# Subtracting, exponentiating and summing the first ten units of an attention on ScalarE, one activation per head

## The chip, the cores and the metric

The kernel runs on one core of a Trainium2 chip. Its engines are TensorE (PE; PEld is its weight load), VectorE (DVE), ScalarE (ACT), GpSimd (POOL) and SyncE (SP), which issues every DMA here. Each engine takes its instructions in the order of its own queue; semaphores hold an instruction until what it needs is there. The metric is the device time of one execution in microseconds (us), the median of three runs.

## The reference

An attention over pooled keys and values feeds two feed-forward layers (q and k come with a spread of 0.8, v of 0.1):

```python
# q, k, v: (8, 8, 576, 64) = batch, heads, tokens, head_dim
k_p = k.reshape(B, H, 72, 8, D).mean(axis=3)
v_p = v.reshape(B, H, 72, 8, D).mean(axis=3)
scores = np.matmul(q, k_p.transpose(0, 1, 3, 2)) / np.sqrt(D)
scores = scores - np.max(scores, axis=-1, keepdims=True)
attn = np.exp(scores)
attn = attn / (np.sum(attn, axis=-1, keepdims=True) + 1e-09)
x = np.matmul(attn, v_p)              # -> (4608, 512) tokens x model
h = x @ w_in;  x = (h * np.cos(h)) @ w_out        # d_ff = 2048
h = x @ w2_in; out = (h * np.clip(h + 3, 0, 6) / 6) @ w2_out
```

## The kernel before

All work is in fp32. Each large matmul is made of three products of parts: a tensor is split in a rounded high part (`xh`, `wh`, `gh`, `pth`) and a low part (`xl`, `wl`, `gl`, `ptl`), so that four matmuls of 128x512 times three products make one step of a layer's half. The weights come as 64-bit words and are turned into fp32 by DVE with four instructions per half (`convert_weights`, L116 to L128), rounded on ACT (L133) and split on POOL (L134).

The attention goes through *units*: 8 batches of 576 tokens, each cut into four units of 128 tokens and one of 64, 40 in all, each with 8 heads of 72 keys. For a unit:

- `unit_q` (L389) turns the queries: four PE transposes and a copy on ACT into `qT` (L395).
- `unit_s` (L401), once for each half of four heads: two score matmuls (L407) into a PSUM bank (`ap_ps`), DVE takes each head's maximum into `mx` (L416) and subtracts it into `e` in SBUF (L418). `mx` and the bank have two buffers each.
- `unit_exp` (L420): one exponent on ACT over all 576 columns of `e` (L423), with the scores' factor 1/(sqrt(64) x 8) as its scale.
- `unit_norm` (L425): DVE sums each head into `sm` (L429), adds 1e-9 (L430) and takes the reciprocal (L431); POOL multiplies (L433) and copies the last columns (L435).
- `unit_pt` (L443) turns `e` on PE (L459), copies the high part on ACT (`pth`, L463) and takes the low part on DVE (`ptl`, L464). `pv` (L485) multiplies with the values (L494) and an ACT copy and a DMA bring the result into `x_d` (L502, L503).

For each batch keys and values are loaded into one buffer (`raw`), summed by eights on DVE or POOL (L334, L338; the values of batch 1 on POOL), and the keys are turned and copied by ACT into `kbd` (`make_kbd`, L345), from which the score matmuls read.

Then come the 144 + 144 *steps* of the feed-forward layers, `gemm1` (L175) into `h`, a chain of ACT and DVE instructions to `g` (in the first layer L185, L195, L196, the sine L199, L209), `gh` (L212), `gl` (L218), and `gemm2` (L237). A step of the first layer begins once the first 512 tokens of `x_d` are there. The attention is a generator in *pieces*; units 0 to 9 or so run before and around the first step, the others between the steps, by a table of goals (`GOFF`). The queues are not in the order of the code: a scheduler sorts the instructions by due times of its own as the program is built, so that a change of one unit moves its neighbours as well.

ACT reads its functions from tables. The sine and the exponent are in different ones, and a load (ACT_TABLE_LOAD) stands ahead of each change; the copies need none.

Of the kernel before, what the change touches and what calls it, by code (L numbers as in the profile page):

```python
# [8 lines left out]
F32 = mybir.dt.float32  # L9
# [3 lines left out]
AF = mybir.ActivationFunctionType  # L13
ALU = mybir.AluOpType
AX = mybir.AxisListType
# [3 lines left out]
POOL = 8  # L19
MAGIC = 12582912.0  # L20
INV_2PI = 1.0 / (2.0 * math.pi)
TWO_PI = 6.283185


def f(ap):
# [4 lines left out]
def tile_kernel(ctx, tc, q, k, v, wi1, wo1, wi2, wo2, ident_d, mask_d, out):  # L30
    nc = tc.nc
    B, H, S, D = q.shape
    NT, DM = out.shape
    P = 128
    N = 512
    SP = S // POOL
# [153 lines left out]
    def chain1(s):  # L190
# [3 lines left out]
        if m == 0:  # L194
# [3 lines left out]
            )  # L198
            nc.scalar.activation(out=g, in_=g, func=AF.Sin, scale=-TWO_PI)  # L199
        else:  # L200
# [65 lines left out]
    ap = actx.enter_context(tc.tile_pool(name="ap", bufs=1))  # L266
# [6 lines left out]
    raw, kp = {}, {}  # L273
    kbd = [ap.tile([P, NP, 2 * SP], F32, name=f"kbd{n}") for n in range(2)]
    NE = 4
    ebuf = [ap.tile([P, H * SP + P], F32, name=f"e{n}") for n in range(NE)]
    raw_t = ap.tile([P, KC, POOL * D], F32, name="raw")
    qm, qT, pts = {}, {}, {}

    def part_of(b, i):  # L280
        return [u1 > i for _, u1 in PARTS[b]].index(True)
# [4 lines left out]
    def piece(kind):  # L286
        turn = turns[kind] = turns.get(kind, -1) + 1
        if started:
            return ps_a.tile([P, N], F32, tag="ap", name="ap_ps", bufs=2)
        tag = SKIND[kind][turn % len(SKIND[kind])]  # L290
        if tag == "ap":
            return ps_a.tile([P, N], F32, tag="ap", name="ap_ps", bufs=2)
        if tag == "h":
            return ps_h.tile([P, N], F32, tag="h", name="h")
        return ps_y.tile([P, N], F32, tag=tag, name=tag)
# [45 lines left out]
    def make_kbd(b, part):  # L341
        kt = kp[b, "k"]
        ps = piece("q")
        kb = kbd[b % 2]
        cp = lambda o, i_: nc.scalar.activation(out=o, in_=i_, func=AF.Copy)  # L345
        if part == 0:
            for c in range(KFULL):
                nc.tensor.transpose(
                    ps[:, c * P : (c + 1) * P], kt[:, c].rearrange("p e d -> p (e d)"), ident
                )  # L350
            full = (KFULL * P) // (2 * SP)
            cp(
                kb[:D, :full, :SP],
                ps[:D, : full * 2 * SP].rearrange("p (j x) -> p j x", x=2 * SP)[:, :, :SP],
            )
            cp(
                kb[D:, :full, SP:],
                ps[D:, : full * 2 * SP].rearrange("p (j x) -> p j x", x=2 * SP)[:, :, SP:],
            )
            o = full * 2 * SP  # L360
            cp(kb[:D, full, :SP], ps[:D, o : o + SP])
            cp(kb[D:, full, SP : KFULL * P - o], ps[D:, o + SP : KFULL * P])
        else:
            nc.tensor.transpose(
                ps[:, :KREM], kt[:KREM, KFULL].rearrange("p e d -> p (e d)"), ident[:KREM, :KREM]
            )
            cp(kb[D:, NP - 1, 2 * SP - KREM :], ps[D:, :KREM])
# [33 lines left out]
    def unit_s(n, half):  # L401
        b, i = divmod(n, NU)
        w = UNITS[i][1]
        ps = piece("s")
        t = qT[n]
        for j in range(2):
            nc.tensor.matmul(  # L407
                ps[:w, j * 2 * SP : (j + 1) * 2 * SP],
                t[:, 2 * half + j, :w],
                kbd[b % 2][:, 2 * half + j, :],  # L410
                start=True,
                stop=True,
            )
        s3 = ps[:w, : 4 * SP].rearrange("p (g s) -> p g s", s=SP)
        mx = ap.tile([P, 4, 8], F32, tag="mx", name="mx", bufs=2)[:, :, 0:1]
        nc.vector.tensor_reduce(out=mx[:w, :, 0], in_=s3, op=ALU.max, axis=AX.X)  # L416
        e = ebuf[n % NE][:w, half * 4 * SP : (half + 1) * 4 * SP].rearrange("p (g s) -> p g s", s=SP)
        nc.vector.tensor_tensor(out=e, in0=s3, in1=mx[:w].to_broadcast([w, 4, SP]), op=ALU.subtract)  # L418

    def unit_exp(n):  # L420
        w = UNITS[n % NU][1]
        e = ebuf[n % NE][:w, : H * SP]
        nc.scalar.activation(out=e, in_=e, func=AF.Exp, scale=1.0 / (math.sqrt(D) * POOL))  # L423

    def unit_norm(n):  # L425
        w = UNITS[n % NU][1]
        e = ebuf[n % NE][:w, : H * SP].rearrange("p (h s) -> p h s", s=SP)
        sm = ap.tile([P, H, 4], F32, tag="sm", name="sm", bufs=2)[:, :, 0:1]
        nc.vector.tensor_reduce(out=sm[:w, :, 0], in_=e, op=ALU.add, axis=AX.X)  # L429
        nc.vector.tensor_scalar(out=sm[:w], in0=sm[:w], scalar1=1e-9, scalar2=None, op0=ALU.add)  # L430
        nc.vector.reciprocal(out=sm[:w], in_=sm[:w])  # L431
        eng = nc.vector if n in ND else nc.gpsimd
        eng.tensor_tensor(out=e, in0=e, in1=sm[:w].to_broadcast([w, H, SP]), op=ALU.mult)  # L433
        e = ebuf[n % NE][:w]
        eng.tensor_copy(  # L435
            out=e[:, H * SP :].rearrange("p (t j x) -> p t j x", t=2, x=VR),
            in_=pairs_of(e)[:, :, P:].unsqueeze(1).to_broadcast([w, 2, NP, VR]),
        )

    def pairs_of(e):  # L440
        return e[:, : H * SP].rearrange("p (j x) -> p j x", x=2 * SP)

    def unit_pt(n):  # L443
# [11 lines left out]
        ps = piece("p")  # L455
        e = ebuf[n % NE][:w]
        kc = NP if w == P else KC
# [49 lines left out]
    def attention():  # L507
        units = B * NU
        normed = finished = 0
        for n in range(units + 3):  # L510
            b, i = divmod(n, NU)
            if n < units:
                unit_s(n, 0)
                yield
                unit_s(n, 1)
                unit_exp(n)
                yield
                if n + 3 < units:
                    load_q(n + 3)
                if n + 1 < units:  # L520
                    unit_q(n + 1)
                    yield
            if n < units and b + 1 < B:
                if i == 2:
                    pool_kv(b + 1, "k", nc.vector if KD[b + 1] else nc.gpsimd)
                    load_kv(b + 1, "v")
                if i == 4:
                    make_kbd(b + 1, 0)
                    yield
                    make_kbd(b + 1, 1)  # L530
                    yield
            while normed < units and n - normed >= NL[normed // NU]:
                unit_norm(normed)
                normed += 1
# [25 lines left out]
    for bl in range(NB):  # L560
        n = NAL[bl]
        steps += [(0, (0, bl), bl, fc, fc == 0, fc == n - 1) for fc in range(n)]
    SA = len(steps)
    for bl in range(NB):
        n = NAL[bl]
# [15 lines left out]
    pool_kv(0, "k", nc.vector, K0S)  # L581
    load_kv(0, "v")
    make_kbd(0, 0)
    make_kbd(0, 1)
    unit_q(0)
# [75 lines left out]
    for slot in range(2 * (T + LAG) + 4):  # L661
# [3 lines left out]
        if not odd and s < T:  # L665
# [9 lines left out]
            if key[0] == 1 and fc == NF - 5:  # L675
                for c in range(NC):
                    t = ypl.tile([P, N], F32, tag="yv", name="yv", bufs=4)
                    nc.sync.dma_start(
                        out=t, in_=yp_d[c * P : (c + 1) * P, bl * N : (bl + 1) * N]
# [95 lines left out]
```

## Time and profile before

| | before |
|---|---|
| median of three runs (lowest to highest) | 1800.62 us (1800.45 to 1802.0) |
| the profiled execution | 1801.62 us |
| its span, first to last instruction | 1799.8 us |
| PE busy | 1739.2 us, 97% |
| DVE / ACT / POOL busy | 896.4 / 891.6 / 393.8 us |
| mean granted TensorE clock | 0.986 of full speed |

A row of the trace names a line, an engine, an operation, and what is written from what is read; then how many, their busy time, the mean of one in ns, and the idle time of the engine just before them with what ended it. Idle time is put down to whatever came last. Engine times overlap, so a sum of busy times is not a time of the program; what an engine's work is worth is read stage by stage.

### The profile page before, as it was taken

The page shows a single profiled execution, that of the slowest core. Times are in us where ns is not written, and L with a number is a line of the kernel's source. Part 1 is how long each engine was busy: PE and PEld are TensorE (multiplying, and loading weights), DVE is VectorE, ACT ScalarE, POOL GpSimd, SP SyncE. Part 2 cuts the span into 40 slices and gives each one's busy share as a digit, 9 for nine tenths or more (in the row PEclk, how much of TensorE's full clock was granted, in tenths as well). Part 3 has the DMA queues.
Part 4 walks back from the last instruction along what each step waited for, and adds up shares of the span by engine and source line. Part 5 has one row for each costly group of instructions (what it writes and reads, how often), then busy time and mean ns, then how long its engine had stood idle before and what let it go on. Part 6 is the DMA issues. An engine that isn't in the chain of part 4 may idle for free.

```text
span 1799.8 us, 21002 instructions
## 1 busy us (share of the span) xinstructions
PE 1739.2 (97%) x7952; PEld 1429.5 (79%) x7952; DVE 896.4 (50%) x1398; ACT 891.6 (50%) x1508; POOL 393.8 (22%) x320
## 2 busy tenths in 40 slices
PE   5689999999999999999999999999999999999999
PEld 4567777788888888888888788888888888888887
DVE  6998656656777656654446852222222222222222
ACT  3588878787666655555556543232323222232222
POOL 2755444222223222221112421010101000010000
PEclk7799999999999999999999999999999999999999
DMA  7656442323333313222223411010101010100000
GB/s 196 194 172 195 143 136 74 118 83 103 117 105 118 106 59 105 97 85 76 71 70 106 140 59 47 1 47 1 47 1 48 0 47 8 40 18 24 0 24 24
DMA packets 115077, 139.84 MB, mean 78 GB/s; under 512 B 44192, under 2 KB 68896, under 8 KB 114976
## 3 DMA queue, kind: packets, MB, share of 16 engines
q1 hardware_dynamic: 114976, 138.51, 24.8%
q8 instruction: 62, 1.02, 0.2%
q14 instruction: 39, 0.32, 0.1%
HBM read 100.73 MB, written 37.75 MB: 77 GB/s over the span
## 4 chain that ended last, share of the span: by engine, by line
PE 85%; DVE 6%; DMA 3%; POOL 2%; ACT 2%; issue 2%; SPq 0%; DVEq 0%; POOLq 0%; ACTq 0%
PE y L237 40%; PE h L175 40%; PE ap_ps L494 1%; PE ap_ps L407 1%; DVE raw L334 1%; DMA raw<-in_k_dram 1%; DMA raw<-in_v_dram 1%; POOL xl L153 1%; DVE sm L429 1%; DVE g L196 1%; POOL e L433 1%; DVE a L125 1%; PE ap_ps L393 0%; PE ap_ps L459 0%; DVE sm L430 0%
## 5 line engine op out<-in xcount | busy, mean ns | idle before, releaser
L175 PE MATMUL h<-xl,wh 128*128 128x512 f32 x1152 | 451.3, 392 | 4.2 <-POOL xl L153 4.2
L175 PE MATMUL h<-xh,wh 128*128 128x512 f32 x1152 | 453.5, 394 | 0.5 <-DVE g L209 0.5
L175 PE MATMUL h<-xh,wl 128*128 128x512 f32 x1152 | 450.8, 391 | 0.0
L201 DVE SCALAR_TENSOR_TENSOR g<-g,h 128x512 f32<-128x512 f32 x144 | 99.3, 689 | 454.7 <-ACT g L187 454.7
L153 POOL TENSOR_TENSOR xl<-xr,xh 128x512 fp32r<-128x512 f32 x108 | 153.3, 1438 | 779.2 <-ACT xh L152 778.1
L187 ACT ACTIVATE g<-h,bias_c 128x512 f32<-128x512 f32 x144 | 99.0, 687 | 409.7 <-PE h L175 409.3
L218 DVE TENSOR_TENSOR gl<-g,gh 128x512 fp32r<-128x512 f32 x255 | 190.3, 746 | 157.7 <-ACT gh L212 154.4
L212 ACT ACTIVATE gh<-g 128x512 fp32r<-128x512 f32 x288 | 181.6, 630 | 175.2 <-DVE g L201 104.5
L175 PEld LDWEIGHTS h<-xl,wh 128*128 128x128 f32 x1152 | 216.7, 188 | 50.2 <-POOL xl L153 6.5
L175 PEld LDWEIGHTS h<-xh,wh 128*128 128x128 f32 x1152 | 216.9, 188 | 45.5 <-issue 1.2
L175 PEld LDWEIGHTS h<-xh,wl 128*128 128x128 f32 x1152 | 216.9, 188 | 44.3
L237 PE MATMUL y<-gh,wh 128*128 128x512 f32 x576 | 226.7, 394 | 0.0
L237 PE MATMUL y<-gl,wh 128*128 128x512 f32 x576 | 226.6, 393 | 0.0
L237 PE MATMUL y<-gh,wl 128*128 128x512 f32 x576 | 225.6, 392 | 0.0
L237 PE MATMUL y<-wh,gh 128*128 128x512 f32 x576 | 224.3, 389 | 1.1 <-DVE yv L245 1.1
L237 PE MATMUL y<-wh,gl 128*128 128x512 f32 x576 | 224.1, 389 | 0.0
L237 PE MATMUL y<-wl,gh 128*128 128x512 f32 x576 | 224.1, 389 | 0.0
L196 DVE SCALAR_TENSOR_TENSOR g<-g,t 128x512 f32<-128x512 f32 x144 | 112.6, 783 | 149.8 <-ACT g L195 149.5
L134 POOL TENSOR_TENSOR wl<-a,wh 128x512 fp32r<-128x512 f32 x64 | 88.4, 1381 | 269.4 <-ACT wh L133 269.4
L237 PEld LDWEIGHTS y<-wh,gh 128*128 128x128 f32 x576 | 108.2, 188 | 24.4 <-DVE yv L245 1.9
L199 ACT ACTIVATE g<-g 128x512 f32<-128x512 f32 x144 | 91.0, 632 | 72.9 <-DVE g L196 72.5
L237 PEld LDWEIGHTS y<-wh,gl 128*128 128x128 f32 x576 | 108.1, 188 | 22.5
(110 smaller groups left out, 2086.1 us busy)
## 6 DMA issues: line engine op xcount, KB each, us to landing
xr<-x_d SPq DMA_DIRECT2D x72, 256.0 KB, 3.2
st<-in_moe_w_in_dram SPq DMA_DIRECT2D x32, 512.0 KB, 6.6
st<-in_moe_w_out_dram SPq DMA_DIRECT2D x32, 512.0 KB, 4.1
yp_d<-ys SPq DMA_DIRECT2D x36, 256.0 KB, 2.4
yv<-yp_d SPq DMA_DIRECT2D x36, 256.0 KB, 3.4
xr<-y_d SPq DMA_DIRECT2D x36, 256.0 KB, 2.7
out_dram<-ys SPq DMA_DIRECT2D x36, 256.0 KB, 2.0
raw<-in_k_dram SPq DMA_DIRECT2D x8, 1024.0 KB, 5.7
```

The source lines that it names most:

```text
L125: nc.vector.scalar_tensor_tensor(out=a, in0=hi, scalar=0xC0000000, in1=a, op0=ALU.bitwise_and, op1=ALU.bitwise_or)
L134: nc.gpsimd.tensor_tensor(out=wl, in0=w, in1=f(wh), op=ALU.subtract)
L153: nc.gpsimd.tensor_tensor(out=xl, in0=t, in1=f(xh), op=ALU.subtract)
L175: nc.tensor.matmul(h, a[:, cs], z, start=(n == 0), stop=(n == 3 * NC - 1))
L187: nc.scalar.activation(out=g, in_=hs[s], func=AF.Relu, bias=bias_c[:, 2:3], scale=1.0)
L196: mark[s] = nc.vector.scalar_tensor_tensor(out=g, in0=g, scalar=MAGIC, in1=t, op0=ALU.subtract, op1=ALU.subtract)
L199: nc.scalar.activation(out=g, in_=g, func=AF.Sin, scale=-TWO_PI)
L201: mark[s] = nc.vector.scalar_tensor_tensor(out=g, in0=g, scalar=6.0, in1=h, op0=ALU.min, op1=ALU.mult)
L212: nc.scalar.activation(out=gh, in_=g, func=AF.Copy)
L218: eng.tensor_tensor(out=gl, in0=gs[s][0], in1=f(gh), op=ALU.subtract)
L237: nc.tensor.matmul(y[c], a, z, start=(first and n == 0), stop=(last and n == 2))
L334: eng.tensor_tensor(out=t[:, :, :w], in0=t[:, :, :w], in1=t[:, :, w : 2 * w], op=ALU.add)
```

## The change

In units 0 to 9 (`HX`) the subtract, the exponent and the sum become one activation for each head, exp(-score + mx) with `mx` as bias column and the sum written into `sm` by the activation itself. An activation can only add its bias, so the scores must come with the other sign: the copies into `kbd` multiply by `S_SCALE` = -1/64 and DVE takes the minimum instead of the maximum, which is the negative maximum. From unit 10 on the subtract, the exponent over 576 columns and the sum stay as they were, with a scale of -1. `sm` has four buffers instead of two, and lives from the first half of the scores on.

```diff
+S_SCALE = -1.0 / 64.0
...
+    HX = range(10)
...
-        cp = lambda o, i_: nc.scalar.activation(out=o, in_=i_, func=AF.Copy)
+        cp = lambda o, i_: nc.scalar.activation(out=o, in_=i_, func=AF.Copy, scale=S_SCALE)
...
-        nc.vector.tensor_reduce(out=mx[:w, :, 0], in_=s3, op=ALU.max, axis=AX.X)
+        nc.vector.tensor_reduce(out=mx[:w, :, 0], in_=s3, op=ALU.min, axis=AX.X)
         e = ebuf[n % NE][:w, half * 4 * SP : (half + 1) * 4 * SP].rearrange("p (g s) -> p g s", s=SP)
-        nc.vector.tensor_tensor(out=e, in0=s3, in1=mx[:w].to_broadcast([w, 4, SP]), op=ALU.subtract)
+        if n in HX:
+            if half == 0:
+                sums[n] = ap.tile([P, H, 4], F32, tag="sm", name="sm", bufs=4)[:, :, 0:1]
+            for g in range(4):
+                nc.scalar.activation(
+                    out=e[:, g],
+                    in_=s3[:, g],
+                    func=AF.Exp,
+                    bias=mx[:w, g],
+                    scale=-1.0,
+                    accum_out=sums[n][:w, half * 4 + g],
+                )
+        else:
+            nc.vector.tensor_tensor(
+                out=e, in0=s3, in1=mx[:w].to_broadcast([w, 4, SP]), op=ALU.subtract
+            )
 
     def unit_exp(n):
+        if n in HX:
+            return
         w = UNITS[n % NU][1]
         e = ebuf[n % NE][:w, : H * SP]
-        nc.scalar.activation(out=e, in_=e, func=AF.Exp, scale=1.0 / (math.sqrt(D) * POOL))
+        nc.scalar.activation(out=e, in_=e, func=AF.Exp, scale=-1.0)
...
-        sm = ap.tile([P, H, 4], F32, tag="sm", name="sm", bufs=2)[:, :, 0:1]
-        nc.vector.tensor_reduce(out=sm[:w, :, 0], in_=e, op=ALU.add, axis=AX.X)
+        if n in HX:
+            sm = sums.pop(n)
+        else:
+            sm = ap.tile([P, H, 4], F32, tag="sm", name="sm", bufs=4)[:, :, 0:1]
+            nc.vector.tensor_reduce(out=sm[:w, :, 0], in_=e, op=ALU.add, axis=AX.X)
```

The scheduler's order on the engines, with the line numbers of each kernel (those of the changed one are larger by 1 to 22), at two places. A name such as e_96 is one of the four buffers of `e`. DVE before, from the first maximum, units 0 and 1:

```order
L416 TENSOR_REDUCE mx<-ap_ps 128x4 x2
L418 TENSOR_TENSOR e_96<-ap_ps,mx 128x288 x2
L416 TENSOR_REDUCE mx<-ap_ps 128x4
L334 TENSOR_TENSOR raw<-raw 128x5x256
L429 TENSOR_REDUCE sm<-e_96 128x8
L334 TENSOR_TENSOR raw<-raw 128x5x128
L430 TENSOR_SCALAR sm<-sm 128x8
L418 TENSOR_TENSOR e_97<-ap_ps,mx 128x288
L338 TENSOR_TENSOR vt<-raw 128x320
L431 RECIPROCAL sm<-sm 128x8
```

and after, at the same place:

```order
L418 TENSOR_REDUCE mx<-ap_ps 128x4 x2
L336 TENSOR_TENSOR raw<-raw 128x5x256
L452 TENSOR_SCALAR sm<-sm 128x8
L418 TENSOR_REDUCE mx<-ap_ps 128x4
L336 TENSOR_TENSOR raw<-raw 128x5x128
L453 RECIPROCAL sm<-sm 128x8
L340 TENSOR_TENSOR vt<-raw 128x320
L418 TENSOR_REDUCE mx<-ap_ps 128x4
```

The subtracts and the sum are gone, and the reciprocal of unit 0 has come ahead of the last sum of the values. ACT before, around unit 9 (e_97, 64 tokens) and the first steps:

```order
L423 ACTIVATE e_97<-e_97 64x576
L185 ACTIVATE t<-h 128x512
L395 ACTIVATE qT<-ap_ps 128x512
L195 ACTIVATE g<-t 128x512
L345 ACTIVATE kbd_94<-ap_ps 64x3x72 x2
L345 ACTIVATE kbd_94<-ap_ps 64x72
L345 ACTIVATE kbd_94<-ap_ps 64x8
L345 ACTIVATE kbd_94<-ap_ps 64x64
L185 ACTIVATE t<-h 128x512
L199 ACT_TABLE_LOAD
L199 ACTIVATE g<-g 128x512
```

and after:

```order
L424 ACTIVATE e_97,sm<-ap_ps,mx 64x72
L186 ACTIVATE t<-h 128x512
L424 ACTIVATE e_97,sm<-ap_ps,mx 64x72
L196 ACTIVATE g<-t 128x512
L424 ACTIVATE e_97,sm<-ap_ps,mx 64x72 x3
L200 ACT_TABLE_LOAD
L200 ACTIVATE g<-g 128x512
L424 ACT_TABLE_LOAD
L424 ACTIVATE e_97,sm<-ap_ps,mx 64x72 x3
L213 ACTIVATE gh<-g 128x512
```

The eight activations of unit 9 are spread over step 0's chain, the last three behind the sine and a second load, ahead of `gh`; the five copies of the keys have moved behind it. In all the queue of ACT holds 52 table loads after and 56 before; PE's queue holds 7795 matmuls in both. From about the 800th of them on PE's order is that of before.

## Rows read from the trace of the kernel before

**Rows 1.** The page: busy tenths in 40 slices of 45 us each.

```profile
PE   5689999999999999999999999999999999999999
...
DVE  6998656656777656654446852222222222222222
ACT  3588878787666655555556543232323222232222
```

**Rows 2.** Busy times by stage, from the span's start; x counts instructions.

```profile
core 0: us, PE busy (x) PEld busy (x) DVE busy (x) ACT busy (x) POOL busy (x), PEclk, DMA share, GB/s
0.00:16.19 16.19, 4.58 (x19) 3.83 (x20) 4.89 (x10) 3.67 (x8) 1.19 (x6) 1.00 0.80 206
16.19:89.37 73.18, 49.89 (x221) 38.57 (x220) 66.40 (x118) 35.25 (x72) 42.83 (x37) 0.72 0.71 193
89.37:200.00 110.63, 97.44 (x507) 76.92 (x508) 96.84 (x161) 90.85 (x164) 65.16 (x56) 0.97 0.56 167
200.00:300.00 100.00, 95.09 (x508) 77.46 (x507) 63.04 (x112) 78.79 (x138) 40.70 (x41) 1.00 0.44 137
300.00:500.00 200.00, 197.23 (x995) 161.44 (x994) 126.32 (x224) 153.34 (x264) 54.68 (x47) 1.00 0.31 99
500.00:1799.80 1299.80, 1295.00 (x5711) 1071.27 (x5709) 538.90 (x777) 529.70 (x865) 189.19 (x136) 1.00 0.17 54
```

**Rows 3.** Waits from 16.19 to 89.37: total us, times, longest us.

```profile
POOL e L433 <- DVE sm L431: 35.3, 5, 22.6
...
ACT wh L133 <- DVE a L128: 10.9, 5, 4.1
PE ap_ps L407 <- DVE e L418: 10.6, 5, 4.5
```

**Rows 4.** DVE by line, 16 to 89.4: busy us, mean ns, idle before.

```profile
L416 DVE TENSOR_REDUCE mx<-ap_ps 128x4 f32<-128x288 f32 (+1 forms) x20 | 8.8, 450 | 8.9 <-PE ap_ps L407 8.8
L418 DVE TENSOR_TENSOR e<-ap_ps,mx 128x288 f32<-128x288 f32 (+1 forms) x20 | 8.5, 447 | 0.1
L429 DVE TENSOR_REDUCE sm<-e 128x8 f32<-128x576 f32 (+1 forms) x10 | 7.4, 744 | 0.5 <-ACT e L423 0.5
L128 DVE SCALAR_TENSOR_TENSOR a<-e,a 128x512 f32<-128x512 bf16 x6 | 6.7, 1122 | 0.0
```

**Rows 5.** Pieces of the timeline: start us, us taken, engine, instruction.

```profile
16.19 0.46 DVE L416 TENSOR_REDUCE mx<-ap_ps 128x4 f32<-128x288 f32 x1 [5.55 <-PE ap_ps L407]
...
24.55 0.91 ACT L379 ACTIVATE vmh<-sph,mask 128x256 fp32r<-128x256 f32 x2
...
47.89 5.55 POOL L334 TENSOR_TENSOR raw<-raw 128x1280 f32<-128x1280 f32 x2
...
49.03 3.01 DVE L128 SCALAR_TENSOR_TENSOR a<-e,a 128x512 f32<-128x512 bf16 x1
...
89.37 0.81 DVE L196 SCALAR_TENSOR_TENSOR g<-g,t 128x512 f32<-128x512 f32 x1 [0.45 <-ACT g L195]
...
101.44 1.28 ACT L423 ACT_TABLE_LOAD   x1 [1.11 <-DVE e L418]
102.73 0.69 ACT L423 ACTIVATE e<-e 128x576 f32<-128x576 f32 x1
```

**Rows 6.** ACT by line and shape, whole run: busy us, mean ns, idle before.

```profile
L187 ACT ACTIVATE g<-h,bias_c 128x512 f32<-128x512 f32 x144 | 99.0, 687 | 409.7 <-PE h L175 409.3
L185 ACT ACTIVATE t<-h 128x512 f32<-128x512 f32 x144 | 85.1, 591 | 73.0 <-PE h L175 72.5
L199 ACT ACT_TABLE_LOAD x28 | 35.9, 1283 | 0.5
...
L423 ACT ACTIVATE e<-e 128x576 f32<-128x576 f32 x32 | 21.9, 684 | 1.3 <-DVE e L418 0.9
L379 ACT ACTIVATE vmh<-sph,mask 128x256 fp32r<-128x256 f32 x16 | 7.6, 502 | 0.6 <-PE ap_ps L494 0.6
...
L345 ACT ACTIVATE kbd<-ap_ps 64x72 f32<-64x72 f32 x6 | 1.3, 224 | 0.1
...
L345 ACT ACTIVATE kbd<-ap_ps 64x8 f32<-64x8 f32 x6 | 1.0, 173 | 0.1
```

More of the change, by code (lines that the diff above doesn't have):

```diff
@@ L275, in tile_kernel @@
     NE = 4
+    HX = range(10)
     ebuf = [ap.tile([P, H * SP + P], F32, name=f"e{n}") for n in range(NE)]
     raw_t = ap.tile([P, KC, POOL * D], F32, name="raw")
-    qm, qT, pts = {}, {}, {}
+    qm, qT, pts, sums = {}, {}, {}, {}
     def part_of(b, i):
```

## Prediction

> **What bounds the kernel now.** I read the 40 slices of the page first, then the busy times by stage. From 300 us on TensorE (PE) is busy 1492.2 of 1499.8 us and nothing but its own work counts [rows 1, 2]. A change to the attention's softmax can therefore move the end only by moving the point at which PE becomes full. All that idles on PE is early: 11.6 us before the first maximum (16.19 us), 23.3 us from there to the first `g` of the feed-forward steps (89.37 us), 13.2 us in the next 110.6 us and 7.7 us from 200 to 500 us [rows 2].
>
> Call the 73.18 us from 16.19 to 89.37 stage B. All ten units that are changed lie in it; beside them DVE converts six halves of weights there and POOL splits and sums [rows 4, 5]. In it VectorE (DVE) is busy 66.40 us, 91%, ScalarE (ACT) 35.25 us, 48%, GpSimd (POOL) 42.83 us, 59%, PE 68% [rows 2]. The longest waits are those of the others for DVE: POOL for the reciprocals on `sm` 35.3 us, ACT for a converted weight 10.9 us, PE for the subtract that frees a score bank 10.6 us [rows 3]. So DVE's queue bounds stage B, and stage B's end sets when the steps begin. It is not a clean bound: from 47.9 to 53.4 us POOL sums values, and a DVE operation that lies beside it takes 3.01 us, where its kind takes 1.12 us on average in this stage [rows 4, 5]. There POOL is as full as DVE.
>
> **What the change takes from DVE.** In ten units both subtracts and the sum go. Stage B holds just these: 20 subtracts, 8.5 us, and 10 sums, 7.4 us [rows 4]. DVE keeps 66.4 - 15.9 = 50.5 us.
>
> The minimum in place of the maximum has the same operands and shape, so I cost it at nothing, as I do the factor in the keys' copies (the same ACT copies, with another constant) and the exponent's factor of -1. PE's matmuls stay 7795 in number, DMA's transfers too.
>
> **What it gives to ACT.** Ten activations of 576 columns go, at 0.684 us 6.8 us, which leaves 35.25 - 6.8 = 28.4 us of other ACT work in B [rows 2, 6]. Eighty activations of 72 columns with a column as bias and an accumulated sum come. None stands in the trace, so I bound one:
> - A copy of 72 columns out of PSUM takes 0.224 us. A bias column costs 0.687 - 0.591 = 0.096 us more at 512 columns. Together 0.320 us [rows 6].
> - Low end: activations that follow each other overlap. Two of 0.502 us each take 0.91 us together, so about 0.09 us is hidden and one costs 0.23 us [rows 5, 6].
> - High end: writing the sum out costs an operation of its own, at the price of the shortest activation here (8 columns, 0.173 us), with nothing overlapped: 0.493 us [rows 6].
>
> I take 0.320, which is built from the two rows nearest to it and lies midway. Eighty cost 18.4, 25.6 or 39.4 us, and ACT in stage B has 46.8, 54.0 or 67.8 us to do. Note what that means: at the middle price ACT, not DVE, is the busiest engine of the stage afterwards.
>
> A rule of the Trainium skill bears on that: ScalarE: Activation LUTs, section What ACT_TABLE_LOAD costs, gives an activation with a column as bias 280 ns + 0.833 ns a column and says that back-to-back ones overlap by 93 ns. For 72 columns that is an estimate of 0.340 us alone and 0.247 us in a row, near my middle and my low price; by 0.247 ACT would have 48.2 us and the stage would end near the low case below. It names no price for the accumulated sum, and no run shown here has one. The rule speaks against cutting one activation into eight, and the trace agrees that the fixed part is large: 8 columns cost 0.173 us of the 0.224 us that 72 cost [rows 6].
>
> **How long stage B is then.** DVE held 91% because all others waited for it. With ACT at 54, DVE at 50.5 and POOL at 42.8 us, each engine hands on to the next and none can be that full. The nearest row for such a balance is the stage behind it (89.37 to 200 us): there ACT is busy 90.85 of 110.63 us, 82%, DVE 87.5%, PE 88% [rows 2]. With ACT at 82% stage B takes 54.0 / 0.82 = 65.9 us, 7.3 us less. DMA would have to carry the stage's 193 GB/s x 73.18 us in that time, 214 GB/s; the start of the program shows 206 GB/s [rows 2], so I cost transfers at nothing, and they would be late first if I am wrong. What is late next is otherwise POOL around the value sums, and ACT.
>
> **Waits that the change adds.** A score bank is free now after a maximum (0.45 us) and a subtract (0.45 us) on DVE; then after the minimum and four activations, 0.45 + 4 x 0.32 = 1.73 us. Over 20 halves that is 16.6 us more of holding, on two banks. Behind the waiting score matmul on PE stand transposes and the P.V products. At most half, 8.3 us, could come onto PE's path; as the bank is waited for 10.6 us now because DVE is late [rows 3], and DVE will be earlier, I take zero. And `mx` has two buffers: the minimum of a half waits for the activations of the half before the last, with the weight conversions queued behind it on DVE. That is also zero as long as ACT keeps up.
>
> The order on ACT changes as well: four activation-table loads fewer, 52 for 56, all behind stage B. A load takes 1.283 us and the exponent starts 0.01 us after it [rows 5, 6], so 5.1 us of ACT's 90.85 us in that next stage go; ACT isn't alone in bounding it, so I count none of it. The skill's same section puts a switch at about 2.66 us, load and drain; by that it would be 10.6 us. The trace has no such drain: 1.28 us stand between the start of the load and that of the exponent. Against the gain, unit 9's last three activations now stand between the sine and `gh` of step 0, behind a load; the copies of the keys that stood there move behind. I count that at nothing.
>
> **Sum.** -7.3 us in stage B, nothing elsewhere. The profiled execution took 1801.62 us (its span 1799.8), which gives 1794.3. The median of the runs is 1.0 us below the profiled one, so the forecast is 1793.3 us.
>
> **The rivals.**
> - *Cheap activations, DVE still the bound.* At 0.23 us ACT has 46.8 us, DVE 50.5. At DVE's 87.5% stage B takes 57.7 us: -15.5, 1785.1 us. For it: the overlap in the rows. Against: POOL's full stretch and the in-order queues. Chance 0.13.
> - *ACT takes DVE's place.* At 0.493 us ACT has 67.8 us; if it holds the 91% that DVE holds now, the stage is 74.8 us: +1.6, 1802.2 us. For it: the sum must leave the accumulator somehow. Chance 0.15.
> - *The gain comes and goes again.* The steps begin 7 us earlier, but from 89 to 200 us PE already idles 13.2 us behind DVE and ACT. If that stage's pace is set by conversions and units 10 and later, of which nothing is removed, most is given back: -1, 1799.6 us. Against: the conversions begin earlier too, and the gain is lost only if they don't. Chance 0.10.
> - *Slower: ACT is the bound and its queue is entangled.* The eight activations of a unit stand in ACT's queue among copies that wait for PE and rounded weights that wait for DVE; the score bank and `mx` then hold PE and DVE back. ACT reaches 82% and has 67.8 us: 82.7 us, +9.5, 1810.1 us. At 82% it decides at (28.4 + 80 p) / 0.82 = 73.18, that is p = 0.395 us for one activation: cheaper is faster than now, dearer slower. Chance 0.20.
> - That the change doesn't do what it says is excluded as far as the order shows it: the eighty activations are there, and the sums and subtracts of ten units aren't.
>
> **Chances and range.** The forecast has 0.42. With the cheap case, 0.55 lie at faster by over 0.2%, 3.6 us, which is about what a measurement of this kernel can tell from no change. ACT in DVE's place and the gain given back make 0.25 for within 0.2%, and 0.20 are left for slower. The range goes from the cheap case, 1785, to 1806, which takes in the pricier cases and about half of the slow one.
>
> **What would show it.** In the changed profile the per-head activation has a mean near 0.32 us, and no row or a short one beside it for the sum. The first `g` stands near 82 us, DVE's busy share from 16 us to there is 75 to 80%, ACT's above 75%, and the waits of PE and POOL for DVE are less than half. PE's idle time behind 89 us (now about 26 us with the end of the run) stays, so that the end moves as the first `g` does. I am wrong if an activation and its sum take over 0.4 us, if score matmuls wait for ACT for more than they waited for DVE, or if the first `g` is earlier and the end isn't.

## The result, and the profile after

The changed kernel is slower: 1809.74 us (1809.21 to 1810.02), where the kernel before took 1800.53 beside it. The ratio is 1.0051, 95% interval 1.0038 to 1.0063. The forecast was 1793.3.

The profiled execution took 1810.02 us, its span 1808.2. Busy times by stage, with the first `g` of the steps (86.72 us) as the second bound; these rows answer to [rows 2]:

```profile
core 0: us, PE busy (x) PEld busy (x) DVE busy (x) ACT busy (x) POOL busy (x), PEclk, DMA share, GB/s
0.00:16.19 16.19, 4.51 (x18) 3.76 (x19) 4.89 (x10) 3.67 (x8) 1.19 (x6) 1.00 0.80 202
16.19:86.72 70.53, 46.53 (x212) 36.95 (x211) 54.89 (x89) 50.23 (x210) 42.75 (x38) 0.70 0.67 189
86.72:200.00 113.28, 96.45 (x483) 73.72 (x482) 95.04 (x152) 81.05 (x160) 59.80 (x52) 0.91 0.58 170
200.00:300.00 100.00, 94.82 (x504) 77.86 (x503) 60.65 (x108) 79.72 (x140) 40.04 (x40) 1.00 0.44 134
300.00:500.00 200.00, 196.44 (x998) 160.46 (x996) 126.95 (x225) 153.62 (x265) 54.58 (x47) 1.00 0.31 96
500.00:1808.20 1308.20, 1303.40 (x5747) 1078.30 (x5745) 543.84 (x785) 535.32 (x875) 191.63 (x138) 1.00 0.17 55
```

Stage B is 70.53 us long instead of 73.18: 2.65 us shorter, not 7.3. DVE's share fell from 91 to 78%, ACT's rose from 48 to 71%. The loss lies in the next stage: up to 200 us PE is busy 96.45 of 113.28 us at a mean granted clock of 0.91, where it was 97.44 of 110.63 at 0.97.

ACT by line and shape, whole run (busy us, mean ns, idle before), answering to [rows 6]:

```profile
L424 ACT ACTIVATE e<-ap_ps,mx 128x72 f32<-128x72 f32 x64 | 19.5, 321 | 7.3 <-DVE sm L452 5.7 <-DVE mx L418 1.4
L442 ACT ACTIVATE e<-e 128x576 f32<-128x576 f32 x24 | 16.4, 684 | 3.4 <-DVE e L433 3.2
L424 ACT ACTIVATION_READ_ACCUMULATOR e<-ap_ps,mx 128x1 f32 x64 | 13.3, 208 | 0.0
L424 ACT ACTIVATE e<-ap_ps,mx 64x72 f32<-64x72 f32 x16 | 4.8, 310 | 2.3 <-DVE mx L418 2.2
```

The activation costs the 0.320 us of the forecast. A read-out of the sum follows each, 0.2 us long, overlapped with its neighbours; the timeline (start, us taken) shows the distance from head to head, 0.30 us:

```profile
16.75 0.32 ACT L424 ACTIVATE e<-ap_ps,mx 128x72 f32<-128x72 f32 x1 [1.06 <-DVE mx L418]
16.97 0.19 ACT L424 ACTIVATION_READ_ACCUMULATOR e<-ap_ps,mx 128x1 f32 x1
17.06 0.31 ACT L424 ACTIVATE e<-ap_ps,mx 128x72 f32<-128x72 f32 x1
17.27 0.20 ACT L424 ACTIVATION_READ_ACCUMULATOR e<-ap_ps,mx 128x1 f32 x1
17.36 0.32 ACT L424 ACTIVATE e<-ap_ps,mx 128x72 f32<-128x72 f32 x1
```

Waits from 16.19 to 86.72 us (total, times, longest), answering to [rows 3]:

```profile
POOL e L455 <- DVE sm L453: 30.6, 6, 22.2
DVE mx L418 <- PE ap_ps L409: 13.1, 6, 5.5
PEld ap_ps L409 <- ACT e L424: 9.0, 5, 4.6
...
PE y L481 <- DVE ptl L486: 6.4, 1, 6.4
ACT e L424 <- DVE sm L452: 5.7, 1, 5.7
...
PE ap_ps L409 <- DVE mx L418: 4.4, 1, 4.4
...
PE ap_ps L409 <- ACT e L424: 3.5, 4, 2.5
```

DVE is busy 11.5 us less than before, and POOL still waits 30.6 us for it, where it waited 35.3. What DVE does beside POOL's value sums takes longer than before [rows 5]. DVE, and then POOL, from 49 to 54 us:

```profile
49.58 2.59 DVE L117 TENSOR_SCALAR a<-st 128x512 uint32<-128x512 uint32 x1 [1.20 <-DMA st<-in_moe_w_in_dram]
52.20 4.18 DVE L121 SCALAR_TENSOR_TENSOR a<-st,a 128x512 uint32<-128x512 uint32 x1
```

```profile
48.99 2.89 POOL L336 TENSOR_TENSOR raw<-raw 128x1280 f32<-128x1280 f32 x1
...
52.28 1.52 POOL L336 TENSOR_TENSOR raw<-raw 128x640 f32<-128x640 f32 x1
53.77 1.25 POOL L135 TENSOR_TENSOR wl<-a,wh 128x512 fp32r<-128x512 f32 x1
```

The wait of PE for `ptl`, 6.4 us, ends with an instruction that stands in DVE's queue behind that 4.18 us. Over the stage this instruction of the conversion, seven times, took (before, then after):

```profile
L120 DVE SCALAR_TENSOR_TENSOR a<-st,a 128x512 uint32<-128x512 uint32 x7 | 6.3, 896 | 0.0
```

```profile
L121 DVE SCALAR_TENSOR_TENSOR a<-st,a 128x512 uint32<-128x512 uint32 x7 | 9.4, 1350 | 0.1
```

Where the rest went is best seen on PE, whose work is the same in both kernels by step 15. I cut the time from 16.2 us to step 15's first activation into windows of 1 us; in each, idle is length less busy, and lost to the clock is busy time x (1 - granted clock), a clock of 0.5 being 1.2 GHz and 1.0 being 2.4 GHz:

| from 16.2 us to step 15 | length | idle | lost to the clock | the rest: work at full clock |
|---|---|---|---|---|
| before | 213.3 | 37.9 | 19.2 | 156.2 |
| after | 220.8 | 42.5 | 21.7 | 156.6 |

The 7.5 us are 4.6 us of idle PE, 2.5 us of half clock and 0.4 us of work. How the time is shared between idle and clock before step 0 shifts from trace to trace: cut_122 and cut_145 below have one and the same order up to there and show 22.5 and 15.2 us, 26.6 and 9.8 us, so there only the sum can be read. From step 0 to step 15, where the clock is mostly full, after takes 10.0 us more than before: 3.7 us of idle, 4.8 us of half clock and 1.5 us of work, most of which before does ahead of step 0. Behind step 15 another 0.9 us comes, up to the 8.4 us between the spans.

### The profile page after: what moved, and what is told of

The parts are those of the page before. It is cut to its first block, busy times and chain, and to the rows that moved or that the text cites. A ratio compares the mean times of both kernels' runs of the same rounds, so it can differ in the third digit from the quotient of the medians.

```text
span 1808.2 us, 21109 instructions
## 1 busy us (share of the span) xinstructions
PE 1742.1 (96%) x7952; PEld 1431.0 (79%) x7952; DVE 886.3 (49%) x1368; ACT 903.6 (50%) x1654; POOL 390.0 (22%) x320
## 4 chain that ended last, share of the span: by engine, by line
PE 85%; DVE 6%; DMA 3%; ACT 3%; issue 1%; POOL 1%; SPq 0%; DVEq 0%; POOLq 0%; ACTq 0%
PE y L238 41%; PE h L176 41%; DMA raw<-in_v_dram 2%; PE ap_ps L516 2%; DVE raw L336 1%; PE ap_ps L409 1%; DMA raw<-in_k_dram 1%; DVE a L121 1%; DVE g L197 1%; POOL xl L154 1%; PE ap_ps L481 0%; ACT e L424 0%; PE ap_ps L395 0%; DVE ptl L486 0%; DVE sm L451 0%
## 5 line engine op out<-in xcount | busy, mean ns | idle before, releaser
L238 PEld LDWEIGHTS y<-gh,wl 128*128 128x128 f32 x576 | 108.6, 189 | 22.3
```

The source lines that it names most:

```text
L238: nc.tensor.matmul(y[c], a, z, start=(first and n == 0), stop=(last and n == 2))
```

## The experiments

A trace is one execution. Executions of one and the same kernel lie up to 5 us apart (1797.1 to 1802.4 us for the kernel before in one series), so verdicts rest on the ratios to the kernel before on the same chip, and the steps' times only say where a difference arises. The row of sign_only, whose order is that of before, shows how far such a time is chance: 0.2 us up to step 8, 1.2 us at step 15. The first activation of a step (`t`, [rows 6]), in us after or before that of the kernel before (87.73, 90.47, 104.28, 145.53, 167.30 and 229.48 us):

| kernel | median us | ratio (95%) | step 0 | 1 | 2 | 5 | 8 | 15 |
|---|---|---|---|---|---|---|---|---|
| after | 1809.7 | 1.0051 (1.0038 to 1.0063) | -2.5 | +2.6 | -2.2 | +5.1 | +6.8 | +7.5 |
| sign_only | 1799.9 | 1.0000 (0.9990 to 1.0009) | -0.2 | -0.2 | -0.2 | -0.2 | -0.2 | -1.2 |
| old_order | 1803.4 | 1.0020 (1.0011 to 1.0030) | +3.0 | +3.0 | +3.0 | +2.2 | +2.2 | +1.2 |
| new_order | 1816.9 | 1.0096 (1.0079 to 1.0112) | +4.3 | +8.4 | +3.6 | +11.3 | +12.9 | +14.0 |
| one_move | 1807.8 | 1.0045 (1.0030 to 1.0060) | -2.5 | +2.4 | -2.5 | +5.1 | +6.8 | +7.1 |
| pool_swap | 1808.4 | 1.0046 (1.0031 to 1.0061) | -2.1 | +2.9 | -1.9 | +2.8 | +5.2 | +5.7 |
| pool_and_xh | 1807.8 | 1.0037 (1.0025 to 1.0049) | -1.7 | +3.3 | -1.6 | +3.8 | +5.5 | +5.9 |
| no_read | 1807.6 | 1.0039 (1.0024 to 1.0054) | -3.2 | +1.7 | -3.1 | +3.4 | +5.9 | +6.5 |
| placed | 1803.5 | 1.0017 (1.0008 to 1.0027) | +3.0 | +3.0 | +3.0 | +2.2 | +2.2 | +1.5 |
| cut_40 | 1803.3 | 1.0022 (1.0012 to 1.0031) | +3.1 | +3.1 | +2.9 | +2.1 | +2.1 | +1.0 |
| cut_60 | 1801.2 | 1.0010 (1.0001 to 1.0020) | -0.2 | -0.2 | +0.2 | -1.5 | -1.5 | -2.7 |
| cut_85 | 1799.7 | 1.0001 (0.9992 to 1.0010) | -1.7 | +1.9 | -0.4 | -0.6 | -0.6 | -1.6 |
| cut_104 | 1801.7 | 1.0010 (1.0001 to 1.0019) | -1.8 | +3.0 | -2.2 | +1.8 | +1.8 | +0.8 |
| cut_122 | 1801.2 | 1.0012 (1.0002 to 1.0021) | -2.4 | +2.5 | -2.3 | +0.2 | +0.2 | -0.5 |
| cut_145 | 1807.6 | 1.0045 (1.0028 to 1.0062) | -3.1 | +2.1 | -2.7 | +7.1 | +5.5 | +4.8 |
| less_dve | 1797.0 | 0.9987 (0.9977 to 0.9996) | -4.3 | -4.3 | -4.4 | -4.4 | -4.4 | -5.2 |
| hx4_old | 1798.4 | 0.9987 (0.9978 to 0.9996) | -1.8 | -1.8 | -1.8 | -3.1 | -3.1 | -3.4 |
| hx4_own | 1803.5 | 1.0019 (1.0009 to 1.0028) | -1.8 | -2.6 | -9.0 | -8.5 | -0.3 | +3.2 |
| hx8_own | 1802.9 | 1.0014 (1.0005 to 1.0024) | -2.6 | -3.3 | -9.8 | -8.8 | -0.8 | +2.1 |

**The order and the work, taken apart.** In most kernels here the order of the instructions on each engine is written out, up to the last place where the two orders differ. The edit is an edge between neighbours in a queue that makes nobody wait:

```diff
+    by = {i.name: i for i in nc.cur_bb.bb.instructions}
+    info = mybir.DependencyInfo(mybir.DependencyClass.NoSync, mybir.DependencyReason.DATA)
+    for names in ORDER:
+        for a, b in zip(names, names[1:]):
+            tc.add_manual_dep(by[f"I-{b}"], f"I-{a}", info, reason="order")
```

*sign_only* is the sign, the minimum and the factor in the keys alone, for which the scheduler makes the same order as before:

```diff
-    HX = range(10)
+    HX = range(0)
```

> Only the sign and the factor: the keys carry -1/64, minimum for maximum, exponent with -1, and no unit takes the new path. Its queues hold the order of the kernel before. Both theories: 1800.6 us, within 1 us. Anything else would mean that the sign or the scale of the copies costs time.

It took 1799.87 us, ratio 1.0000: these parts cost nothing. *old_order* is the whole edit with the instructions that both kernels have in the order of before and the eighty activations where they fit; *new_order* is the work of before, subtracts and sums included, in the order of after.

> The edit of the first ten units is whole, but all instructions that both kernels have stand in each queue in the order of the kernel before; only the eighty new activations find their place in between. Theory 'order' (the loss is the order that the scheduler gave to the neighbours, above all around the start of the second block): 1793 to 1800 us, since DVE still loses 15.9 us of work in the first 89 us. Theory 'price' (eighty activations and their sums fill ACT's queue, and score banks are held longer): it has the same activations, so 1806 to 1812 us.

> The reverse: the computation of the kernel before (subtract, exponent and sum as they were), its shared instructions in the order of the changed kernel; subtracts, exponents and sums of the first ten units find their place in between. Theory 'order': as slow as the changed kernel or slower, 1807 to 1816 us. Theory 'price': no activation is added, so near the kernel before, 1799 to 1803 us.

With the order of before the edit is 0.20% slower than the kernel before, with its own 0.51%; the work of before in the order of after is 0.96% slower. So the order of after is bad for either kernel, by 0.31% or 5.6 us with the edit and 17.3 us without. The edit is worth 8.1 us in that order (0.96 less 0.51%), about what was forecast, and costs 3.6 us in the order of before. old_order lies between its two expectations, new_order just above the one of 'order'. In each of the two runs the scheduler found places for the instructions that the order's own kernel doesn't have, and these places are part of the differences.

**Where the order loses.** The first guess was ScalarE's queue, in which the eighth high half of x waited behind a `qT` copy. *one_move* moves that one instruction:

```diff
 ACT
+L153 ACTIVATE xh<-xr (8th part of x)
 L397 ACTIVATE qT<-ap_ps (unit 14)
 ...
-L153 ACTIVATE xh<-xr (8th part of x)
```

> The changed kernel with its whole order held, and one instruction of ACT moved: the fourth rounding copy of the second block's x (which started at 146.8 us) stands five places earlier, ahead of the query copy that made ACT wait 8.2 us for PE. Theory 'order': 4 to 8 us of the 8.4 us come back, 1801 to 1805 us. Theory 'price': the place of one copy changes little, 1808 to 1810 us.

The high half came at 137.89 instead of 146.81 us and step 5 at 150.65, as in after (150.66). The late half did not hold the step. Then I used cuts: all that starts in the trace of after before a time T keeps its order, the rest stands as in the kernel before.

```diff
-ORDER = the order of before
+ORDER = the order of after for what starts before T; the order of before for the rest
```

> The changed kernel's computation whole. On every engine the order is that of the changed kernel for all that started in its trace before 85.3 us (step 0's first activation), and that of the kernel before for the rest; the seven activations of unit 9 that are left stand behind the g of step 0. Theory (the loss is made after step 0, by the order there, as TensorE pauses and the half clock behind them): step 0 comes at 85 to 86 us as in the changed kernel, the pauses of 1.74 and 2.32 us at 136 to 141 us are gone, and the later steps stay 1 to 2.5 us ahead of the kernel before: 1797.5 to 1800. Rival (the loss is in what stage B leaves undone: TensorE did 1.0 us less of its work by step 0, other engines likewise, and this comes due in any order): the later steps fall 3 us or more behind, 1803 or more.

> As the cut at 85.3 us, with the changed kernel's order kept for all that started before 104 us (past the sine of steps 0 and 1 with their extra table loads), then that of the kernel before. If the loss is made after 104 us by the order there: 1798 to 1800.5. If the steps 0 and 1 of the changed order (table loads, weight work moved ahead, 3.1 us less of TensorE's work between steps 0 and 2) make it: 1803 or more.

> As the cut at 104 us (1801.7), with the changed kernel's order kept for all that started before 122 us. If the order between 104 and 122 us adds to the loss, 1803 or more; if the loss beyond the first two steps is that of the start of block 1 alone (the pauses at 136 to 141 us and steps 5 and 6), 1801 to 1802.5.

> As the cut at 122 us, at 145 us, past the pauses of 1.74 and 2.32 us at 136 to 141 us and the half clock behind them. Theory (these pauses and the half clock make most of the loss): 1806 to 1809. Rival (steps 5 to 8 behind them make it): 1803 or less.

With the cut at 85 us the edit takes as long as the kernel before (1.0001), at 104 and 122 us 0.10 and 0.12% longer, at 145 us 0.45%. So most of the loss, some 6 us, arises from the order between 122 and 145 us, and some 2 us from that of the first two steps (the intervals of cut_85 and cut_104 overlap). cut_104 lies between its two expectations, cut_122 and cut_145 lie where the pauses were expected to put them. The theory on cut_85 was right and its rival, that stage B leaves work undone which comes due in any order, wrong; but the edit then brings nothing.

TensorE in two stretches of the place, for before, after, cut_122 and cut_145 in this order (length, busy, granted clock, DMA share, GB/s):

```profile
core 0: us, PE busy (x), PEclk, DMA share, GB/s
136.00:140.50 4.50, 4.03 (x22) 1.00 0.28 91
140.50:148.00 7.50, 6.42 (x37) 1.00 0.57 176
```

```profile
136.00:140.50 4.50, 1.11 (x4) 1.00 0.49 175
140.50:148.00 7.50, 6.83 (x22) 0.54 0.50 162
```

```profile
136.00:140.50 4.50, 4.50 (x25) 1.00 0.50 148
140.50:148.00 7.50, 6.42 (x37) 1.00 0.55 175
```

```profile
136.00:140.50 4.50, 0.96 (x3) 0.92 0.47 168
140.50:148.00 7.50, 7.12 (x25) 0.59 0.53 174
```

In the order of after PE stands still for 3.4 of the 4.5 us, and once it goes on it runs for some 7 us near the half clock; that is another 3 us lost (6.83 x 0.46). PE's and POOL's timeline in after shows what PE waited for:

```profile
137.90 0.50 PE L176 MATMUL h<-xl,wh 128*128 128x512 f32 x1 [1.74 <-POOL xl L154]
...
141.18 0.80 PE L176 MATMUL h<-xl,wh 128*128 128x512 f32 x1 [2.32 <-POOL xl L154]
```

```profile
132.71 1.17 POOL L455 TENSOR_TENSOR e<-e,sm 128x576 f32<-128x576 f32 x1 [4.59 <-DVE sm L453]
133.84 1.28 POOL L154 TENSOR_TENSOR xl<-xr,xh 128x512 fp32r<-128x512 f32 x1
135.06 1.56 POOL L457 COPY e<-e 128x128 f32<-128x128 f32 x1
136.59 1.26 POOL L154 TENSOR_TENSOR xl<-xr,xh 128x512 fp32r<-128x512 f32 x1
137.81 1.85 POOL L219 TENSOR_TENSOR gl<-g,gh 128x512 fp32r<-128x512 f32 x1
139.61 1.51 POOL L154 TENSOR_TENSOR xl<-xr,xh 128x512 fp32r<-128x512 f32 x1
```

PE's queue has the matmuls of step 5 almost in a row there, and they wait for low halves of x that stand on POOL between a copy of `e`, a `gl` and a multiplication for which POOL had waited 4.59 us. In cut_122 PE does `y` matmuls of earlier steps, scores and the first matmuls of step 6 in that time. *pool_swap* moves two of these halves, *pool_and_xh* the eighth high half as well:

```diff
 POOL
 L154 xl (5th part of x)
+L154 xl (6th part)
 L457 COPY e (unit 12)
-L154 xl (6th part)
+L154 xl (7th part)
 L219 gl (step 4)
-L154 xl (7th part)
```

> The changed kernel with its own order on every engine written out, and two low halves of x (the 6th and the 7th, made by GpSimd for step 5) put ahead of a copy of unit 12 and of the low half of g of step 4. Theory (PE pauses): TensorE sat idle 1.74 us and 2.32 us before these two low halves at 136 to 141 us, then its granted clock was 0.5 from 140.7 to about 147 us, which costs another 3.3 us; with both halves some 1.5 us earlier the pauses shrink to under 1 us each, the clock stays at 1.0 for more of the stretch, and step 5's first activation comes 1 to 2 us before 150.65, no more, because the 8th low half still waits at 147.5 behind the high half that the trace of the single move showed. Time 1806 to 1808.5. Rival (the pauses are not what costs): step 5's first activation stays within 0.5 us of 150.65 and the time at 1809 to 1810.

> As the one before, and the high half of the 8th x part put ahead of the qT copy of unit 14 on ScalarE (the move that alone gave 1807.8). Theory (PE pauses and the late 8th part together): step 5's first activation moves from 150.65 to about 146 us, the granted clock between 140 and 148 us is 1.0, the offset of the later steps falls from +7.5 to about +3 and the time to 1803 to 1805. Rival (something else holds step 5): 1807 or more, with step 5 at 149.5 us or later.

pool_swap gave step 5 2.4 us earlier than in after and 1808.4 us, at the upper end of the theory's range; the intervals of the two ratios overlap, so no gain is shown, and the pauses were 1.50 and 1.08 us, not under 1. pool_and_xh missed: step 5 at 149.33, 1807.8 us, not 1803 to 1805. POOL shows why the order of two halves isn't enough (pool_and_xh, POOL, then DVE):

```profile
134.50 3.76 POOL L154 TENSOR_TENSOR xl<-xr,xh 128x512 fp32r<-128x512 f32 x2
138.21 0.88 POOL L457 COPY e<-e 128x128 f32<-128x128 f32 x1
139.06 1.27 POOL L154 TENSOR_TENSOR xl<-xr,xh 128x512 fp32r<-128x512 f32 x1
```

```profile
135.15 2.00 DVE L336 TENSOR_TENSOR raw<-raw 128x1280 f32<-128x1280 f32 x1
```

The second half, now beside DVE's sum of values, took 2.5 us instead of 1.27, and PE still waited 1.5 and 0.6 us. With the pauses halved to 2.1 us the loss to the clock between steps 2 and 8 stayed at the 4.8 us of after. No run moved the multiplication for which POOL waited.

That the order between 122 and 145 us makes most of the loss is shown by the cuts. The pauses and the clock behind them come and go with it and are large enough: from step 0 to step 15 cut_145 takes 5.9 us more than cut_122, with 2.1 us more idle, 5.2 us more lost to the clock and 1.5 us less work. A cure by single moves is not shown.

**What stage B's work is worth.** *no_read* takes the sums' output away in the order of after, *less_dve* takes work from DVE in the order of before:

```diff
-                    accum_out=sums[n][:w, half * 4 + g],
...
             sm = sums.pop(n)
+            src = e[:, :, 0:1]
...
-        nc.vector.tensor_scalar(out=sm[:w], in0=sm[:w], scalar1=1e-9, scalar2=None, op0=ALU.add)
+        if n not in HX:
+            src = sm[:w]
+        nc.vector.tensor_scalar(out=sm[:w], in0=src, scalar1=1e-9, scalar2=None, op0=ALU.add)
```

```diff
-        nc.vector.tensor_reduce(out=mx[:w, :, 0], in_=s3, op=ALU.max, axis=AX.X)
+        few = s3[:, :, :8] if n < 10 else s3
+        nc.vector.tensor_reduce(out=mx[:w, :, 0], in_=few, op=ALU.max, axis=AX.X)
...
-        nc.vector.tensor_reduce(out=sm[:w, :, 0], in_=e, op=ALU.add, axis=AX.X)
+        few = e[:, :, :8] if n < 10 else e
+        nc.vector.tensor_reduce(out=sm[:w, :, 0], in_=few, op=ALU.add, axis=AX.X)
```

> The changed kernel with its own order written out; the eighty activations leave out their sums (no accumulator output), and the normalisation takes each head's first exponential in the place of the sum, so the output is not the softmax. It tells what the sums' output costs. Theory (the read-out is hidden, as the pitch of 0.295 us with 0.32 us of activation and 0.20 us of read-out suggests, but not fully): pitch 0.23 to 0.25 us per head, ScalarE 4 to 5 us less busy in the stretch 16.19 to 89.37 us, first steps up to 1 us earlier, time within 2 us of 1809.7. Rival (the activations' price is what makes the changed kernel late): the time falls by 5 us or more.

> The kernel before, with its own order written out on every engine; in the first ten units the maxima and the sums are taken over 8 of each head's 72 columns, so the output is not the softmax's. It takes VectorE work out of stage B (some 8 us by the rows of the 128x288 and 128x576 reductions, less what a short reduction still costs) and gives none to another engine. Theory of the prediction (VectorE bounds stage B, its length is VectorE's busy time over a share that stays): step 0's first activation 6 to 9 us before 87.73 us, the time at 1791 to 1794. Rival (no engine bounds stage B: it is a chain through all engines, and a relieved engine waits more): step 0 comes 0.5 to 3 us earlier, time 1797 to 1800.

Without the sums a head follows the last after 0.203 us instead of 0.295 (medians of the distances), 7.4 us of ACT for eighty and more than expected; step 0 came 0.8 us earlier than in after and the time fell by 0.12%, within the intervals. So the price of the read-outs is not what makes the changed kernel late. DVE by line in less_dve from 16.19 to 89.37 us, to be held against [rows 4]:

```profile
L417 DVE TENSOR_REDUCE mx<-ap_ps 128x4 f32<-128x32 f32 (+1 forms) x19 | 3.4, 183 | 3.6 <-PE ap_ps L407 3.4
...
L431 DVE TENSOR_REDUCE sm<-e 128x8 f32<-128x64 f32 (+1 forms) x10 | 2.1, 212 | 0.8 <-ACT e L424 0.8
```

That is 20 x 0.267 + 10 x 0.532 = 10.7 us less in these two rows, and no work more on another engine. By step 0 DVE is busy 57.8 us in all, where it was 65.2: other instructions of its queue took longer. Step 0 came 4.3 us earlier, between the two expectations, and the kernel is 0.13% faster, 2.3 us, near what the rival had. DVE's share up to step 0 falls from 91 to 86%, so the length did not follow its busy time. PE's idle time and its loss to the clock, together, are 35.0 us before step 0 by the same cutting as above, 38.9 before. A microsecond taken off DVE's rows is worth 0.4 us at step 0 here, one of ACT, in the order of after, about 0.1 (0.8 of 7.4).

**Why the order of before loses with the edit.** *placed* is old_order with the activations of units 4, 8 and 9 behind the ACT instructions that others wait for; cut_40 and cut_60 keep the order of after for the first 40 or 60 us; *hx4_old* is the edit in four units in the order of before.

```diff
 ACT
-L424 ACTIVATE e<-ap_ps,mx x8 (unit 4)
 L524 ACTIVATE xs<-y x2
+L424 ACTIVATE e<-ap_ps,mx x4 (unit 4)
 L524 ACTIVATE xs<-y
+L424 ACTIVATE e<-ap_ps,mx x4 (unit 4)
 ... (units 8 and 9 likewise)
```

```diff
-    HX = range(10)
+    HX = range(4)
```

> The changed kernel's computation with the order of the kernel before on every engine (that gave 1803.4 with the activations wherever they fell), and now the activations of unit 4 behind the first two and the third copy of the pooled output, those of unit 8 behind the first two high halves of x, and the second four of unit 9 behind a square of the weight conversion. Theory (queue places: the activations stood ahead of ScalarE's work that others waited for): the copies of the pooled output come at 46.5 instead of 49.06 us, step 0 at 87 to 88.5 instead of 90.74 us, and the time is 1799 to 1801.5. Rival (the price of the activations on ScalarE itself makes the 3 us): step 0 stays at 90 us or later, the time at 1802.5 or more.

> As the cut at 60 us, at 40 us. With the whole order of the kernel before the same computation took 1803.4 and step 0 came at 90.74 us. Theory (queue places after 40 us make those 3 us): step 0 still at 89 to 91 us, 1802 to 1804. Rival (the first four units' places make them): step 0 at 88 us or earlier, 1800.5 or less.

> As the cut at 85.3 us, with the changed kernel's order kept only for what started before 60 us, then that of the kernel before; the activations of the units behind that stand where the scheduler puts them. Theory (the gain of stage B belongs to the changed order's placing of ScalarE's and VectorE's work throughout the stage): less is gained than with the cut at 85.3 us, step 0 at 86 to 89 us, 1799 to 1802. Rival (the first 60 us hold it all): as the cut at 85.3 us within 0.7 us.

> The edit in the first four units only (32 activations in the place of 8 subtractions, 4 exponentials and 4 sums), the order of the kernel before on every engine. Theory (what the edit costs in that order is ScalarE's added time behind 40 us, in units 4 to 9, where its copies are waited for): step 0 at 86.5 to 88 us, time 1797.5 to 1800. Rival (every unit's activations cost alike): step 0 at 88.5 to 89.5 us, 1800 to 1802.

placed brought the first `xs` from 49.06 to 47.20 us, but step 0 stayed at 90.75 and the time at 1803.45, so these three places do not make the 3 us. Nor does the rival, the activations' price by itself: cut_60 has the same eighty activations, and step 0 is back at 87.52 us, while cut_40 changes nothing. So the order between 40 and 60 us decides. hx4_old is faster than both kernels: 1798.43 us, 0.9987 (0.9978 to 0.9996). So units 0 to 3 gain 2.3 us in the order of before, and units 4 to 9 lose 5.9 (from -0.13 to +0.20%). Which instruction of the order between 40 and 60 us loses them was not taken apart.

Last, the orders that the scheduler makes for four and for eight units by itself (`HX = range(4)` and `range(8)`, nothing else):

> The edit in the first four units, in the order that the scheduler makes of it. The order moves of itself; the theory that the order carries the result says only that the time stands or falls with TensorE's pauses and half clock up to step 8: if step 8's first activation is within 2.5 us of 167.30 us, the time is 1798 to 1802.5; if it is 5 us or more late, 1805 or more.

> The edit in the first eight units, so that no activation stands between the sine and the low half of step 0, in the order that the scheduler makes of it. The same reading as for four units: the offset of step 8 from 167.30 us is the time's offset from the kernel before within 2 us, and 1800 to 1812 is all that can be said ahead.

They are slower than the kernel before by 0.19 and 0.14%, and so than hx4_old. Both expectations missed: step 8, by which I meant to read them, was within 1 us of before, and the loss came between steps 8 and 15 in both. Where it comes from there was not looked into. hx4_own and hx4_old do the same work; 5.1 us lie between their medians.

## Why the prediction was wrong

**What was right.** The price of a head: 0.295 us measured, 0.320 taken, both under the 0.395 us that I gave as deciding. That it came so near is in part luck: the 0.320 left out the read-out of the sum (0.092 us) and the overlap of neighbours (0.118 us), which nearly cancel. By that price alone both rivals with a dear activation were out, and the slower side came all the same. The sign and the factor cost nothing (sign_only), and PE's matmuls are as many as before (7952 records in each trace; the queue was counted at 7795). ACT's work in stage B was put at 54.0 us and was 50.2.

The Trainium skill, ScalarE: Activation LUTs, section What ACT_TABLE_LOAD costs, led to an estimate of 0.247 us for such activations in a row; no_read shows 0.203 us, and the measurement decides.

**The step that failed first: "-7.3 us in stage B, nothing elsewhere".** The second half of it is the larger error. I had seen that PE's order differs over the first 800 matmuls and that unit 9's last activations come in between, behind a second load, and counted it at nothing. The order behind 85 us costs 0.50%, 9 us (1.0051 against 1.0001 for cut_85). PE's idle time behind the first `g`, which was to stay at 26 us, is 30.4 us. I had shown the order at DVE's and ACT's changed places only; most of the loss is on PE and POOL at 133 to 148 us, where no instruction of the edit stands, and it grows by the half clock that follows a pause.

**The second: stage B's length as the busiest engine's work over a share of 82%.** It gave 65.9 us and was 70.5, with ACT at 71% and DVE at 78%: 2.65 us less than before, not 7.3. DVE's 91% had been read as a bound. less_dve shows that it wasn't one: 10.7 us off its rows move step 0 by 4.3 us and the end by 2.3. For PE the stretch up to step 0 is 32.6 us of work, 15.9 us lost to the clock and 23.1 us of idle before, and 31.6, 13.5 and 24.0 after: idle and clock together fell by 1.5 us only. DVE's freed time was eaten in part by its own instructions beside POOL's sums: it is busy 54.9 us where 50.5 were forecast, and L121 alone took 9.4 us for seven, 6.3 in the kernel before. And it matters where ACT's new work stands: the edit in the order of before is 3.6 us slower, in its first four units alone 2.3 us faster, and cut_60 wins 3.2 us of step 0 over old_order with the same activations.

**The waits costed at zero.** The score bank: PE's weight loads waited 9.0 us and its matmuls 3.5 us for the activations, where the matmuls had waited 10.6 us for the subtracts, so zero was near. The four table loads fewer were counted at nothing; no run takes them apart.

**The rivals.** "The gain comes and goes again" was nearest by its course: the steps began 2.5 us earlier and the gain was gone within a step. Its reason, the pace of the conversions and of the later units, is not what the cuts show, and it allowed for giving back and not for losing more. The slower case gave 1810.1, close to the result, by a mechanism that was not there: ACT was not the bound. What would have shown me wrong had been named: the first `g` earlier and the end not.

## What to carry to other kernels

Where a scheduler sorts the instructions, compare two kernels in one fixed order before you judge an edit: here the order alone is worth 6 to 17 us and the edit -8 to +4 us, depending on the order. An engine that is busy 91% of a stage with many cross waits need not be its bound; take a known amount of work off it and look how far the next stage moves. Read the predicted order on the engine that is full later, PE here, for any place where its next matmul waits for a part that a slow engine makes late, and count a pause like the 3.4 us here twice, once as idle time and once for the clock behind it.

## What the runs showed of the hardware

- The sum of an activation leaves by an instruction of its own, 0.19 to 0.25 us, overlapped with the activations around it: 0.295 us from head to head of 72 columns with it, 0.203 without.
- Instructions of DVE and POOL take longer beside the value sums of the other engine: an instruction of DVE's weight conversion, 0.9 us on average in the kernel before, took 4.18 us, a low half of 1.27 us on POOL took 2.5, a copy of 0.3 to 0.4 us on POOL took 1.56.
- After a stretch of 4.5 us with 1.1 us of work PE's granted clock was 0.54 over the next 7.5 us, though it was busy 6.83 of them; in before and in cut_122, which do not pause there, it stayed at 1.00.
